# Placing the decoding of the second layer's weights: one or two units behind each f-tile's low part

## The chip, the cores and the metric

The kernel runs on one core of one Trainium2 chip. The metric is the device time of one execution in microseconds, as a median of several. TensorE (PE) does the matrix products, VectorE (DVE), ScalarE (ACT) and GpSimd (POOL) the elementwise work, and SyncE (SP) issues the transfers.

## The reference

Three stages follow one another. The first is attention with a hash mask (2 batches, 8 heads, 768 positions, head size 64). The second and the third are two gated layers over the 1536 resulting tokens of width 512:

```python
a = x @ w1            # 512 -> 1024
b = x @ w2
x = (a * b @ w3) @ w_out          # first layer; back to 512
gate = sigmoid(x @ w_gate)        # 512 -> 1536
val = x @ w_val
out = gate * val @ w_out2         # second layer; back to 512
```

The inputs are 64-bit floats. Each weight comes to the chip as raw 64-bit words and is turned into a 32-bit float there; this is called decoding.

## The kernel before

**Products.** A product of nearly 32-bit precision is made of three matmuls: each operand is split in a high and a low part, and `three` (line 698) sums high by high, high by low and low by high. A weight is split by `split_w` (line 686): ScalarE copies the high part, GpSimd (for the two first-stage weights) or VectorE (for the second-stage weight, `wt`) subtracts to get the low part.

**The loop.** During attention a generator already does the first layer for the first 512 tokens. The function `moe` (line 716) does the rest in 52 f-tiles, numbered n here: tiles 0 to 7 and 8 to 15 are the first layer for the second and third 512 tokens (8 f-tiles each), tiles 16 to 51 the second layer, 12 f-tiles for each 512 tokens. In its program order a tile n issues 12 matmuls into the PSUM tile `pa`, 12 into `pb`, then the split of its second-stage weight (line 786), and `post` (line 733): ScalarE copies `pa` into `a` (a sigmoid in the second layer, line 739), VectorE multiplies `pb` by it (line 741), ScalarE copies the high part `gh` (line 743), VectorE subtracts to get the low part `gl` (line 744). Then come the 12 matmuls of the second stage of the tile before, `second(n - 1)`, into four accumulators called `m` (line 793). At the end of each 512 tokens of the first layer, `second` also moves the four accumulators out, by ScalarE (line 763) and VectorE (line 764) into the tiles `x`. Last come this tile's decodes (lines 794 and 795) and the split of the first-stage weights of tile n + 1 (line 797).

**Decoding.** A unit is 128 by 512 weights. `decode` (line 323) first issues the load of the next unit on SP (`stage_next`, lines 310 to 321; four staging buffers `st` in two pools), and then for its own unit two ScalarE instructions (lines 334 and 335), one GpSimd instruction (line 336) and three VectorE instructions (lines 337, 338 and 343). Its work tiles `da` and `dr` have two buffers each in `moe`. The second layer has 36 units: 12 of `w_gate`, whose results go into the space of `xall`, then 12 pairs of `w_val` and `w_out2`, whose results go into the space of the first layer's weights, `w1r`, `w2r` and `wc`, once these are used up. Tile 16 + i of the second layer needs unit i of `w_gate` and pair i. The function `decodes(n)` gives two units to each odd n and one to each even n up to 24, 36 in all.

**Order.** The attention part is put in order by `order_engines`. The instructions of `moe` are put in order by the framework's scheduler: it simulates the program, and each engine takes the ready instruction that was written first. An instruction of `decode` can so be queued ahead of older work that is not ready yet, as far as its buffers allow. The order that comes out is fixed in each engine's queue, and each queue is worked off in order on the chip.

Of the kernel before, what the change touches and what calls it, by code (L numbers as in the profile page):

```python
# [16 lines left out]
ALU = mybir.AluOpType  # L17
# [211 lines left out]
def lsh_attention_moe_moe2_kernel(  # L229
# [36 lines left out]
    NF2 = FF2 // P  # L266
# [3 lines left out]
    dve = nc.vector  # L270
# [4 lines left out]
    def act_copy(dst, src):  # L275
        act.activation(out=dst, in_=src, func=AF.Copy)  # L276

    def f(ap):
        return ap.bitcast(F32)
# [27 lines left out]
    late = {}  # L307
    alt = [0, 0]

    def stage_next():  # L310

        if units:
            dst, src = units.pop(0)
            alt[0] += 1
            other = late.get("mp") or (wp if "mw" not in late else dec)
            t = (other if alt[0] % 2 else dec).tile([P, CH], U64, tag="st", name="st", bufs=2)
            shp = dst.shape
            ld = sync.dma_start(out=t if len(shp) == 2 else t.rearrange("p (k f) -> p k f", k=shp[1]), in_=src)
            if "c0" in late and alt[0] == 3:
                Tiles.holds.append((ld.ins.name, late["c0"].name))  # L320
            staged.append((dst, t))

    def decode():


        stage_next()
        dst, t = staged.pop(0)
        w = t[:, :].bitcast(U32).rearrange("p (n t) -> p n t", t=2)
        lw, hw = w[:, :, 0], w[:, :, 1]
        alt[1] += 1  # L330
        tp, nb = (late["mp"], 2) if "mp" in late else (wp if "mw" not in late and alt[1] % 2 else dec, 1)
        a = tp.tile([P, CH], U32, tag="da", name="da", bufs=nb)
        r = tp.tile([P, CH], I32, tag="dr", name="dr", bufs=nb)
        act.activation(out=f(a), in_=f(hw), func=AF.Abs)  # L334
        act.activation(out=r, in_=lw, func=AF.Copy, scale=2.0 ** -29)
        pool.tensor_scalar(out=f(a), in0=f(a), scalar1=F64_HI, scalar2=F64_LO, op0=ALU.min, op1=ALU.max)  # L336
        dve.tensor_scalar(out=a, in0=a, scalar1=3, scalar2=0x3FFFFFFF, op0=ALU.logical_shift_left, op1=ALU.bitwise_and)  # L337
        dve.scalar_tensor_tensor(out=a, in0=hw, scalar=0xC0000000, in1=a, op0=ALU.bitwise_and, op1=ALU.bitwise_or)  # L338
        ai, ri = a.bitcast(I32), r
        if len(dst.shape) == 3:  # L340
            ai = ai.rearrange("p (k f) -> p k f", k=dst.shape[1])
            ri = ri.rearrange("p (k f) -> p k f", k=dst.shape[1])
        dve.tensor_tensor(out=dst.bitcast(I32), in0=ai, in1=ri, op=ALU.add)  # L343
# [337 lines left out]
    def split_x(s, t, kcs):  # L681
        for kc in kcs:
            act_copy(t[0][:, kc], xraw[s][:, kc])
            dve.tensor_tensor(out=t[1][:, kc], in0=xraw[s][:, kc], in1=f(t[0][:, kc]), op=ALU.subtract)

    def split_w(pl, nm, src, bufs=2, eng=pool):
        hi = pl.tile([P, DM], F32R, tag=nm + "h", name=nm + "h", bufs=bufs)
        lo = pl.tile([P, DM], F32R, tag=nm + "l", name=nm + "l", bufs=bufs)
        shp = src.shape
        h3, l3 = hi, lo  # L690
        if len(shp) == 3:
            h3 = hi.rearrange("p (k f) -> p k f", k=shp[1])
            l3 = lo.rearrange("p (k f) -> p k f", k=shp[1])
        act_copy(h3, src)
        eng.tensor_tensor(out=l3, in0=src, in1=f(h3), op=ALU.subtract)  # L695
        return hi, lo
# [7 lines left out]
    def stage1(ps, w, x, kcs):  # L704
        for kc in kcs:
            three(ps, [t[:, kc * P:(kc + 1) * P] for t in w], [t[:, kc] for t in x], kc == 0, kc == KC - 1)

    def ftile(fi):

        ck, o = divmod(fi, KC)  # L710
        g = xall[:, o, ck * CH:(ck + 1) * CH].rearrange("p (k f) -> p k f", k=KC)
        if fi < NF1:
            return g, late["w1"][fi], late["w2"][fi].rearrange("p k f -> p (k f)")
        return g, wc[:, fi - NF1].rearrange("p (k f) -> p k f", k=KC), wc[:, fi - NF1 + KC]

    def moe(psM):


        tiles = [(1, s, fi) for s in range(1, NSW) for fi in range(NF1)] + [(2, s, fi) for s in range(NSW) for fi in range(NF2)]
        mp, mw = late["mp"], late["mw"]  # L720
        x2 = [(late["xh"], late["xl"])]
        x2 += [[mp.tile([P, KC, CH], F32R, name=f"x2_{i}_{t}") for i in range(2)] for t in range(1, NSW)]
        split_x(1, x2[1], range(KC))

        def weights(n):

            if n >= len(tiles):
                return None
            m, s, fi = tiles[n]
            ga, gb = (late["w1"][fi], late["w2"][fi]) if m == 1 else ftile(fi)[:2]  # L730
            return [split_w(mp, "wa", ga), split_w(mp, "wb", gb)]

        def post(n, ps):
            m, s, fi = tiles[n]
            a = mp.tile([P, CH], F32, tag="a", name="a", bufs=2)
            if m == 1:
                act_copy(a, ps[0])
            else:
                act.activation(out=a, in_=ps[0], func=AF.Sigmoid)
            gl = mw.tile([P, CH], F32R, tag="gl0", name="gl", bufs=2)  # L740
            dve.tensor_tensor(out=ps[1], in0=ps[1], in1=a, op=ALU.mult)  # L741
            gh = mw.tile([P, CH], F32R, tag="gh0", name="gh", bufs=2)
            act_copy(gh, ps[1])
            dve.tensor_tensor(out=gl, in0=ps[1], in1=f(gh), op=ALU.subtract)
            return gh, gl

        def second(n, g, wt, acc):
            m, s, fi = tiles[n]
            nf = NF1 if m == 1 else NF2
            last = n == len(tiles) - 1  # L750
            mm = None
            for c in range(4):
                cs = slice(c * P, (c + 1) * P)
                with tc.issue_after(mm.ins) if last and c else nullcontext():
                    if m == 1:
                        mm = three(acc[c], [t[:, cs] for t in wt], g, fi == 0, fi == nf - 1)
                    else:
                        mm = three(acc[c], [t[:, cs] for t in g], wt, fi == 0, fi == nf - 1)
            if fi < nf - 1:
                return  # L760
            for c in range(4):
                if m == 1:
                    act_copy(x2[s][0][:, c], acc[c])
                    dve.tensor_tensor(out=x2[s][1][:, c], in0=acc[c], in1=f(x2[s][0][:, c]), op=ALU.subtract)
                else:
                    o = mp.tile([P, DM], F32, tag="a" if last and c < 2 else "o", name="o", bufs=2)
                    if last and c % 2:
                        dve.tensor_copy(o, acc[c])
                    else:
                        act_copy(o, acc[c])  # L770
                    b, n = divmod(s * (CH // P) + c, NT)
                    sync.dma_start(out=out[b * S:(b + 1) * S].rearrange("(p c) d -> c p d", c=NT)[n], in_=o)

        ops = {0: weights(0), 1: weights(1)}
        gs, wts = {}, {}
        acc = None
        for n in range(len(tiles) + 1):
            if n < len(tiles):
                ps = [psM.tile([P, 512], F32, tag=t, name=t) for t in ("pa", "pb")]
                x = x2[tiles[n][1]]  # L780
                w = ops.pop(n)
                for kcs in ([range(KC)] if n else [range(KC - 1), range(KC - 1, KC)]):
                    for i in range(2):
                        stage1(ps[i], w[i], x, kcs)
                m, s, fi = tiles[n]
                wts[n] = split_w(mp, "wt", wc[:, fi] if m == 1 else ftile(fi)[2], eng=dve)
                gs[n] = post(n, ps)
            if n == 0:
                continue
            if acc is None:  # L790
                acc = [psT.tile([P, 512], F32, tag="t", name="m0"), psT.tile([P, 512], F32, tag="t", name="m1"),
                       psT.tile([P, 512], F32, tag="t", name="m2"), psT.tile([P, 512], F32, tag="t", name="m3")]
            second(n - 1, gs.pop(n - 1), wts.pop(n - 1), acc)
            for _ in range(decodes(n)):
                decode()
            if n + 1 < len(tiles):
                ops[n + 1] = weights(n + 1)
            if n == 3:
                split_x(2, x2[2], range(KC))

    def decodes(n):
        return 1 + n % 2 if n <= 24 else 0

    load_head(0, "qk")
    sync.dma_start(out=pq_raw[0:D], in_=proj)
# [126 lines left out]
```

## Time and profile before

| | us |
|---|---|
| median of 3 runs (843.55 to 844.79) | 844.46 |
| the profiled execution's own time | 844.29 |
| its span, from the first to the last instruction | 842.2 |
| PE busy / DVE busy / ACT busy / POOL busy in the span | 805.5 / 568.6 / 524.4 / 337.5 |

The profile was taken of one execution. Its rows name a line of the kernel, an engine, the operation and its tiles (output, then inputs). A matmul row names the moving operand first and the stationary one second. "Idle before" is the time for which an engine stood still ahead of an instruction, with what ended it. Stretches of time are counted from the start of the span.

### The profile page before, as it was taken

How to read it: one execution, taken by the hardware profiler on the slowest of the kernel's cores; microseconds unless marked ns; L12 is line 12 of the kernel's file. 1: busy time of each engine (PE TensorE's matmuls, PEld its weight loads, DVE VectorE, ACT ScalarE, POOL GpSimd, SP SyncE). 2: the span in 40 equal slices, each digit the busy share in tenths (PEclk: the TensorE clock that was granted, in tenths of full speed). 3: DMA queues.
4: the chain of work that ended last, by engine and by line, in shares of the span. 5: the costliest groups of instructions: out<-in, count | busy, mean ns of one | idle time of the engine just before them, and what ended most of it. 6: DMA issues, size and time to landing. Idle time of an engine off the chain costs nothing.

```text
span 842.2 us, 12220 instructions
## 1 busy us (share of the span) xinstructions
PE 805.5 (96%) x4272; PEld 682.6 (81%) x4272; DVE 568.6 (68%) x969; ACT 524.4 (62%) x1024; POOL 337.5 (40%) x329
## 2 busy tenths in 40 slices
PE   6889999999989999999999999999999999999998
PEld 5767878889878989888888677778888888888886
DVE  7999998888899889988399999962222222222222
ACT  5898877677788988777266765653334333343332
POOL 3466332142456352339444455443233333323330
PEclk9999999999999999999999999999999999999999
DMA  7666554344345444322024434300001000010001
GB/s 233 172 165 172 158 159 125 93 110 110 74 126 146 131 118 117 98 61 69 32 72 154 156 120 142 110 0 1 1 1 50 2 1 0 1 51 1 0 1 50
DMA packets 44748, 71.15 MB, mean 84 GB/s; under 512 B 6096, under 2 KB 32720, under 8 KB 44688
## 3 DMA queue, kind: packets, MB, share of 16 engines
q1 hardware_dynamic: 44688, 70.39, 28.7%
q8 instruction: 33, 0.54, 0.3%
q14 instruction: 27, 0.22, 0.1%
HBM read 52.43 MB, written 3.19 MB: 66 GB/s over the span
## 4 chain that ended last, share of the span: by engine, by line
PE 69%; DVE 15%; ACT 8%; issue 6%; DMA 1%; POOL 0%; DVEq 0%; ACTq 0%; POOLq 0%
PE pa L701 13%; PE m L701 12%; PE pb L701 12%; PE av L540 6%; PE tp L523 5%; PE p L701 4%; PE wacc L596 4%; PE s L469 3%; DVE da L338 3%; PE s L472 3%; DVE da L337 3%; PE y L701 3%; DVE pt L527 2%; PE gps L403 2%; ACT e L490 2%
## 5 line engine op out<-in xcount | busy, mean ns | idle before, releaser
L741 DVE TENSOR_TENSOR pb<-pb,a 128x512 f32<-128x512 f32 x52 | 36.2, 696 | 138.8 <-PE pb L701 134.8
L523 PE MATMUL tp<-idf,e 128*128 128x128 f32 x576 | 102.8, 276 | 5.5 <-DVE pt L527 4.3
L490 ACT ACTIVATE e<-s,sm 128x768 f32<-128x768 f32 x96 | 95.9, 999 | 15.2 <-DVE sm L480 13.0
L527 DVE TENSOR_TENSOR pt<-tp,pt 128x384 fp32r<-128x384 f32 x192 | 101.3, 549 | 5.9 <-ACT pt L526 4.3
L526 ACT ACTIVATE pt<-tp 128x384 fp32r<-128x384 f32 x192 | 90.5, 495 | 21.2 <-PE tp L523 19.3
L695 POOL TENSOR_TENSOR wal<-xall,wah 128x512 fp32r<-128x512 f32 x36 | 46.9, 1302 | 136.4 <-ACT wah L276 136.4
L336 POOL TENSOR_SCALAR da<-da 128x512 f32<-128x512 f32 x76 | 52.5, 692 | 119.3 <-ACT da L334 118.7
L701 PE MATMUL pa<-x,wah 128*128 128x512 f32 x320 | 99.3, 389 | 0.0
L479 DVE TENSOR_REDUCE s<-s 128x1 f32<-128x768 f32 x96 | 91.8, 956 | 11.0 <-PE s L472 10.8
L701 PE MATMUL pb<-x,wbh 128*128 128x512 f32 x320 | 98.5, 389 | 0.0
L523 PEld LDWEIGHTS tp<-idf,e 128*128 128x128 f32 x576 | 71.7, 141 | 17.6 <-DVE pt L527 5.8
L540 PE MATMUL av<-pt,spv 128*128 128x256 f32 x576 | 78.5, 286 | 1.0 <-DVE pt L527 0.9
L540 PEld LDWEIGHTS av<-pt,spv 128*128 128x128 f32 x576 | 72.0, 191 | 4.2 <-DVE pt L527 1.4
L334 ACT ACTIVATE da<-st 128x512 f32<-128x512 f32 x76 | 51.3, 675 | 37.6 <-DVE w1r L343 14.2
L469 PE MATMUL s<-ak,aq 128*128 128x384 f32 x192 | 62.1, 388 | 10.6 <-ACT e L490 10.5
L701 PEld LDWEIGHTS pa<-x,wah 128*128 128x128 f32 x320 | 60.1, 188 | 12.4
L701 PEld LDWEIGHTS pb<-x,wbh 128*128 128x128 f32 x320 | 60.1, 188 | 12.4
L338 DVE SCALAR_TENSOR_TENSOR da<-st,da 128x512 uint32<-128x512 uint32 x76 | 67.2, 884 | 1.5
L596 PE MATMUL wacc<-wo,t 128*128 128x512 f32 x192 | 65.4, 417 | 0.1
L701 PE MATMUL pa<-x,wal 128*128 128x512 f32 x160 | 62.3, 389 | 0.0
L701 PE MATMUL pb<-x,wbl 128*128 128x512 f32 x160 | 62.3, 389 | 0.0
L276 ACT ACTIVATE wah<-xall 128x512 fp32r<-128x512 f32 x36 | 22.8, 633 | 56.3 <-PE pa L701 56.2
(161 smaller groups left out, 1930.2 us busy)
## 6 DMA issues: line engine op xcount, KB each, us to landing
st<-in_moe_w_dram SPq DMA_DIRECT2D x32, 512.0 KB, 3.7
st<-in_moe_w_out_dram SPq DMA_DIRECT2D x20, 512.0 KB, 3.4
st<-in_moe_w_gate_dram SPq DMA_DIRECT2D x12, 512.0 KB, 3.5
st<-in_moe_w_val_dram SPq DMA_DIRECT2D x12, 512.0 KB, 3.5
rawq<-in_q_dram SPq DMA_DIRECT2D x16, 192.0 KB, 3.3
rawk<-in_k_dram SPq DMA_DIRECT2D x16, 192.0 KB, 3.3
rawv<-in_v_dram SPq DMA_DIRECT2D x16, 192.0 KB, 2.8
rr<-row SPq DMA_DIRECT2D x16, 192.0 KB, 3.3
```

Of the source, the lines that this page charges most:

```text
L334: act.activation(out=f(a), in_=f(hw), func=AF.Abs)
L336: pool.tensor_scalar(out=f(a), in0=f(a), scalar1=F64_HI, scalar2=F64_LO, op0=ALU.min, op1=ALU.max)
L338: dve.scalar_tensor_tensor(out=a, in0=hw, scalar=0xC0000000, in1=a, op0=ALU.bitwise_and, op1=ALU.bitwise_or)
L469: pe.matmul(s[:, half, :HS], lhsT=m["aq"][:, qs], rhs=m["ak"][:, ks], start=True, stop=False)
L479: dve.tensor_reduce(out=one[:, 1:2], in_=s[:, :, :HS], op=ALU.max, axis=AX.XY, negate=True)
L490: act.activation(out=e.rearrange("p (a c) -> p a c", a=2), in_=s[:, :, :HS], func=AF.Exp, bias=sm[:, 1:2], scale=sm[:, 0:1], accum_out=su_ ...
L523: pe.transpose(ps[:, j * P:(j + 1) * P], e[:, c * P:(c + 1) * P], idf)
L526: act.activation(out=dh, in_=src, func=AF.Copy)
L527: dve.tensor_tensor(out=lo[:, g % 2, half * 3:half * 3 + 3], in0=src, in1=f(dh), op=ALU.subtract)
L540: pe.matmul(acc[:, :2 * P].rearrange("p (a t) -> p a t", a=2), lhsT=w, rhs=r[:, :, c], start=(c == 0 and i == 0), stop=(c == NT - 1 and i ...
L596: pe.matmul(acc, lhsT=t3[x][:, j], rhs=wo[y][:, j], start=(j == 0 and n == 0), stop=(j == NF1 - 1 and n == 2))
L701: mm = pe.matmul(ps, lhsT=lhs[x], rhs=rhs[y], start=start and n == 0, stop=stop and n == 2)
```

## The change

The VectorE instruction that makes the low part `gl` of tile n is remembered. The decodes of tile n are traced in a block that orders each of their VectorE instructions behind it in VectorE's queue (an order of issue, not a wait for its end). The ScalarE, GpSimd and SP instructions of the decodes get no such edge. The number of decodes becomes one for tiles 1 to 12 and two for tiles 13 to 24, 36 in all again, in the same order of units.

```diff
-            dve.tensor_tensor(out=gl, in0=ps[1], in1=f(gh), op=ALU.subtract)
+            late["gl"] = dve.tensor_tensor(out=gl, in0=ps[1], in1=f(gh), op=ALU.subtract).ins
...
-            for _ in range(decodes(n)):
-                decode()
+            with tc.issue_after(late["gl"]):
+                for _ in range(decodes(n)):
+                    decode()
...
     def decodes(n):
-        return 1 + n % 2 if n <= 24 else 0
+
+        return 1 if n <= NF2 else 2 if n <= 2 * NF2 else 0
```

`NF2` is 12.

## Rows read from the trace of the kernel before

**Rows 1.** The page: busy time of the engines over the span.

```profile
PE 805.5 (96%) x4272; PEld 682.6 (81%) x4272; DVE 568.6 (68%) x969; ACT 524.4 (62%) x1024; POOL 337.5 (40%) x329
```

**Rows 2.** Busy time by stretches (header line names the columns).

```profile
core 0: us, PE busy (x) PEld busy (x) DVE busy (x) ACT busy (x) POOL busy (x), PEclk, DMA share, GB/s
426.10:470.00 43.90, 43.87 (x193) 35.86 (x192) 42.73 (x58) 28.14 (x51) 20.43 (x22) 1.00 0.43 135
470.00:558.20 88.20, 82.96 (x351) 64.50 (x350) 82.85 (x105) 56.83 (x103) 47.20 (x43) 1.00 0.34 112
558.20:838.40 280.20, 280.20 (x1237) 231.72 (x1235) 72.16 (x104) 104.77 (x177) 82.69 (x64) 1.00 0.02 9
```

**Rows 3.** Waits of PE, 426 to 558 us (us in total, times, longest).

```profile
PE m L701 <- DVE gl L744: 3.1, 5, 1.4
PE m L701 <- DVE x L764: 1.1, 1, 1.1
```

**Rows 4.** VectorE in order of time, 508 to 517 us (start, us, instruction).

```profile
508.05 0.69 DVE L741 TENSOR_TENSOR pb<-pb,a 128x512 f32<-128x512 f32 x1
508.65 0.68 DVE L343 CUSTOM_DVE_ANT_0 w2r<-da,dr 128x1024 uint16<-128x1024 uint16 x1
509.91 0.69 DVE L744 TENSOR_TENSOR gl<-pb,gh 128x512 fp32r<-128x512 f32 x1 [0.58 <-ACT gh L276]
510.52 0.68 DVE L695 TENSOR_TENSOR wtl<-wc,wth 128x512 fp32r<-128x512 f32 x1
511.12 0.84 DVE L337 TENSOR_SCALAR da<-da 128x512 uint32<-128x512 uint32 x1
511.99 0.69 DVE L338 SCALAR_TENSOR_TENSOR da<-st,da 128x512 uint32<-128x512 uint32 x1
512.60 1.52 DVE L337 TENSOR_SCALAR da<-da 128x512 uint32<-128x512 uint32 x1
514.15 1.66 DVE L338 SCALAR_TENSOR_TENSOR da<-st,da 128x512 uint32<-128x512 uint32 x1
...
516.34 0.69 DVE L741 TENSOR_TENSOR pb<-pb,a 128x512 f32<-128x512 f32 x1
```

**Rows 5.** The chain that ended last, around 564 us (start, us, what).

```profile
563.68 2.72 PE m L701 x12
```

**Rows 6.** VectorE in order of time, 563 to 568 us.

```profile
563.77 0.70 DVE L741 TENSOR_TENSOR pb<-pb,a 128x512 f32<-128x512 f32 x1 [4.01 <-issue]
565.14 0.69 DVE L744 TENSOR_TENSOR gl<-pb,gh 128x512 fp32r<-128x512 f32 x1 [0.67 <-ACT gh L276]
```

**Rows 7.** VectorE in order of time, single instructions at 437 and at 489 to 551 us.

```profile
437.41 0.41 DVE L337 TENSOR_SCALAR da<-da 128x512 uint32<-128x512 uint32 x1
...
489.83 0.69 DVE L741 TENSOR_TENSOR pb<-pb,a 128x512 f32<-128x512 f32 x1
...
499.24 0.69 DVE L741 TENSOR_TENSOR pb<-pb,a 128x512 f32<-128x512 f32 x1
...
551.47 1.19 DVE L343 CUSTOM_DVE_ANT_0 wc<-da,dr 128x1024 uint16<-128x1024 uint16 x1
```

**Rows 8.** GpSimd in order of time, 511 to 516 us.

```profile
511.04 0.63 POOL L336 TENSOR_SCALAR da<-da 128x512 f32<-128x512 f32 x1 [1.24 <-ACT da L334]
512.13 1.70 POOL L695 TENSOR_TENSOR wal<-w1r,wah 128x512 fp32r<-128x512 f32 x1 [0.46 <-ACT wah L276]
...
561.54 1.29 POOL L695 TENSOR_TENSOR wal<-xall,wah 128x512 fp32r<-128x512 f32 x1 [3.80 <-ACT wah L276]
```

**Rows 9.** Waits of SP's queue, 400 to 600 us (total, times, longest).

```profile
SPq L318 <- DVE da L338: 128.3, 31, 30.8
```

**Rows 10.** ScalarE in order of time, 546 to 548 us.

```profile
546.20 0.67 ACT L334 ACTIVATE da<-st 128x512 f32<-128x512 f32 x1 [1.42 <-DVE wc L343]
...
547.98 1.28 ACT L739 ACT_TABLE_LOAD   x1
```

## The prediction

> **What bounds the kernel now.** I began with the page: PE is busy for 805.5 us of 842.2 [rows 1], so the gain has to be sought where PE stands still. That share is too kind, because a matmul's modelled end overlaps the next one; I therefore counted matmuls per stretch instead of reading busy time. From 558.20 us to the end of the loop PE runs 1237 matmuls in 280.20 us, 0.2265 us each [rows 2]. That is its full pace: a tile of 36 matmuls takes 8.15 us, and the chain there consists of PE alone, a dozen matmuls each 2.72 us [rows 5]. At this pace the 351 matmuls of the stretch from 470 to 558.2 us would take 79.5 us; they took 88.2 [rows 2]. The 193 of the stretch before it would take 43.7 us and took 43.9. So decoding costs PE 8.7 + 0.2 = **8.9 us**, nearly all of it in some ten tiles, and nothing later.
>
> Who holds PE there? Its own waits name VectorE: the second stage `m` waits for `gl` five times and for the accumulators' move-out [rows 3]. VectorE is busy for 82.85 of the 88.2 us, against 72.16 of 280.2 us later [rows 2]. I then read one whole VectorE cycle [rows 4]. From one product on `pb` to the next it takes 8.29 us, holding two decode units (each one instruction of lines 337, 338 and 343) and the tile's own three instructions. In the quiet stretch a tile's product starts as soon as `pb` is done and `gl` ends 2.06 us later (563.77 to 565.83) [rows 6]. The second stage of that tile begins only three dozens of matmuls after 563.68, at 571.84 [rows 5]. VectorE can therefore run 6.0 us late before PE feels it. In the stretch of the loss that allowance is used up: two tiles took 9.41 us (489.83 to 499.24) and 8.81 us (499.24 to 508.05) on VectorE [rows 4, 7].
>
> **The change, part by part.** I take its parts against the profiled execution of 844.29 us, 0.17 us below the median of 844.46.
>
> *What stays.* The 36 units, their 36 loads and their order stay; only their place changes. Today the last unit ends at 552.7 us [rows 7]. From 563.68 us to the loop's end at 838.40 lie 274.7 us, 101 dozens of matmuls [rows 2, 5]: tile 17's `m`, three dozens for each of 33 more tiles, and tile 51's `m`. The `gl` that ends at 565.83 [rows 6] is therefore tile 18's, and tile 24's would end six tiles later, near 615 us by today's clock: decoding is spread over 60 us more, at a lower density.
>
> *Tiles 1 to 12, one unit.* VectorE's own work is 2.06 us from product to `gl`, plus 0.68 us for the low part of `wt` [rows 4, 6]. A unit that meets nobody takes 0.41 + 0.69 + 0.68 = 1.8 us [rows 4, 7]. That makes 4.5 us. If VectorE waited out every GpSimd instruction of the tile, two splits of 1.29 us and one clamp of 0.63 us [rows 8], it would be 7.7 us. Both ends are below 8.15 us, so nothing is lost here, not even with the move-out of tile 8 (four instructions of `gl`'s size, 2.8 us), which the 6.0 us cover.
>
> *Tiles 13 to 24, two units.* This is the unknown. The low end of a VectorE cycle is 2.06 + 0.68 + 3.6 = 6.3 us. The high end adds every GpSimd instruction, two splits and two clamps, 3.8 us: 10.1 us. The nearest row is the cycle that already holds two units, 8.29 us; its stretched instructions (0.84 and 1.52 us for line 337, 1.66 us for line 338, against 0.41 and 0.69) carry 2.5 us of such waiting [rows 4, 7]. I take 8.3 us. With c for the cycle, VectorE falls behind by c - 8.15 a tile, and once by 2.8 us for the move-out in tile 16; PE loses 12 x (c - 8.15) + 2.8 - 6.0 us, or nothing if that is negative. At 8.3 us the lag ends at 4.6 us, inside the allowance. The loss starts at c = 8.42.
>
> The stretching is two engines taking turns: a split lasts 1.70 us where VectorE decodes beside it, 1.29 us where it doesn't [rows 8]. The Trainium skill, SBUF — State Buffer, section "SBUF: two separate sides", has GpSimd and some VectorE instructions share a port that one holds to its end while the other is fully blocked. By that rule, if every GpSimd instruction met a decode, c would be the high end; the trace agrees that such waits happen, but shows 2.5 us of them and not 3.8.
>
> *What is queued behind the new edges.* The next tile's product stands behind two units on VectorE. For `gh` ScalarE waits for that product, then `gl`, then PE: this is the chain whose lateness the 6.0 us cover. The edge binds a unit to its own tile's `gl` only, so its last instruction may still fill the pause while ScalarE makes the next `gh`, as in [rows 4].
>
> *Other queues.* SP's 36 loads wait for staging buffers that line 338 frees, 128.3 us in all [rows 9]; they will wait longer, and nobody for them, as four buffers run ahead. ScalarE's two and GpSimd's one instruction per unit follow their two work buffers; they can be done while VectorE handles the tile's own work. If that cover is gone, VectorE waits for them, which is inside the 9.41 us cycle.
>
> *Deadlines.* Pair i is decoded in tile 13 + i and split for tile 16 + i, two tiles or 16 us later; the `w_gate` units have more. No stall of PE should come from here.
>
> *Sum.* 844.46 - 8.9 = 835.6. I leave 0.5 us for the move-out in tile 16, half of the 1.1 us that it cost PE before [rows 3], since it still meets two units: **836.1 us**. This case reaches from 834.6 (nothing lost, and the 0.9 us by which the fastest of the runs shown lies below their median) to 838 (the whole 1.1 us, and a tenth of a microsecond in each of the 12 tiles).
>
> **The rivals.**
> 1. *VectorE stays the bound in the two-unit tiles, and part of the gain is lost.* At c = 8.81 the loss is 4.7 us: 840.3. For it: that cycle stands in the trace with about two units. Against it: it was measured while VectorE was at the end of its allowance and held by full buffers.
> 2. *The same collision, worse, on the other side: slower.* Place: VectorE's queue in tiles 13 to 24, where GpSimd's splits meet two units in each tile. It decides at c = 9.16 us, where the loss reaches 8.9. At 9.41 us the loss is 11.9 us, 847.5; at the high end of 10.1 us it is 20 us, 856. For it: one cycle of 9.41 us with about two units [rows 7]. Against it: the following cycles shrink to 8.81 and 8.29 us.
> 3. *ScalarE must swap tables.* The sigmoid's table load comes at 547.98 us, after the last decode's absolute value at 546.20 [rows 10]; now nine tiles (16 to 24) hold both. ScalarE is busy for 56.83 us in 351 matmuls, 9.75 tiles [rows 2]: 5.8 us a tile. Two loads of 1.28 us a tile make 8.4 us, which the allowance absorbs; four make 10.9 us and lose 9 x 2.75 - 6 = 19 us: 854. No row shows an absolute value after the sigmoid's table, but copies go on under it with no further load. The Trainium skill, ScalarE: Activation LUTs, section "Table sets: the hidden batching unit", counts abs among the cheap functions that every set has; by that there is no swap.
> 4. *The change doesn't do what it says.* If the scheduler's order hardly moved, the time would be 844.5. Against it: the last unit cannot end at 552.7 us any more.
>
> **How the numbers follow.** Forecast 0.75, rival 1 0.12, rival 2 0.05, rival 3 0.02, rival 4 0.06 (with what else may eat the gain). The range takes the forecast's own lower edge, 834.6, and reaches through rival 1, to 841.0. A measurement of this kernel can tell about 0.2%, 1.7 us. Faster by more than that: forecast and rival 1, 0.87. Within it: 0.06. Slower: rivals 2 and 3, 0.07.
>
> **What would show it.** Right: PE in dozens of 2.72 us from 426 us on, no waits of `m` for `gl`; VectorE's busy share in the stretch up to 515 us falling to about two thirds, then high until some 610 us; products in tiles 13 to 24 starting ever later than `pb`'s end, but less than 6 us. Wrong: waits of `m` for `gl` between 515 and 615 us, VectorE cycles above 8.4 us there, more than two table loads on ScalarE, or PE waiting for a split weight in tiles 16 to 27.

## The result, and the profile after

| | before | after |
|---|---|---|
| median of 6 runs each, us | 844.75 (843.55 to 847.65) | 835.75 (834.55 to 837.17) |
| the profiled execution's own time / its span, us | 844.29 / 842.2 | 834.55 / 832.6 |

The ratio is 0.9885, with a 95% interval of 0.9869 to 0.99: 9.0 us less by the medians, against 8.4 us forecast and 8.9 us that the prediction gave as the most to be had. The next line is the page's busy time after, which answers to [rows 1].

```profile
PE 801.0 (96%) x4272; PEld 683.6 (82%) x4272; DVE 540.7 (65%) x969; ACT 523.9 (63%) x1024; POOL 332.0 (40%) x329
```

No instruction was added or taken away on any engine, yet VectorE is busy for 27.9 us less than before: its instructions became shorter. Where they did is seen below. Busy time by stretches, of the changed kernel, answers to [rows 2] and has its columns; the cuts are at 515 us, where the one-unit tiles end, and at 620 us, after the last unit.

```profile
426.10:470.00 43.90, 43.90 (x195) 36.38 (x194) 26.57 (x42) 23.71 (x41) 16.25 (x17) 1.00 0.25 80
470.00:515.00 45.00, 45.00 (x200) 37.25 (x200) 21.72 (x36) 24.88 (x44) 19.06 (x18) 1.00 0.19 63
515.00:620.00 105.00, 105.00 (x465) 86.96 (x464) 72.33 (x115) 63.22 (x113) 50.08 (x49) 1.00 0.30 101
620.00:829.00 209.00, 208.79 (x922) 172.57 (x920) 53.82 (x79) 78.37 (x132) 60.64 (x47) 1.00 0.03 12
```

The matmul counts, in brackets behind PE's busy time, say it all for PE: 860 matmuls in the first 193.9 us are 0.2255 us each, the full pace; before, the 351 from 470 to 558.2 us took 0.2513 us each [rows 2]. (A matmul that runs across a cut is counted on both sides of it; taken as one stretch the 193.9 us hold 857, 0.2263 us each.) VectorE's share is 0.61, 0.48, 0.69 and 0.26 in the four stretches; before it was 0.97 and then 0.94 up to 558 us [rows 2]. PE has no wait at all between 420 and 630 us, so nothing answers to [rows 3]. The chain that ended last (the work followed back from the last instruction) holds nothing but PE from 424 to 620 us:

```profile
by line: PE m L701 35.0%; PE pb L701 34.7%; PE pa L701 30.3%
```

VectorE in order of time, of the changed kernel, answers to [rows 4]: a two-unit tile on time (13), then the product and `gl` of tile 17, behind the move-out, and one of the later tiles (21).

```profile
513.38 0.70 DVE L741 TENSOR_TENSOR pb<-pb,a 128x512 f32<-128x512 f32 x1 [3.72 <-PE pb L701]
514.74 0.69 DVE L744 TENSOR_TENSOR gl<-pb,gh 128x512 fp32r<-128x512 f32 x1 [0.67 <-ACT gh L276]
515.35 0.75 DVE L337 TENSOR_SCALAR da<-da 128x512 uint32<-128x512 uint32 x2
516.02 1.29 DVE L338 SCALAR_TENSOR_TENSOR da<-st,da 128x512 uint32<-128x512 uint32 x2
517.22 0.69 DVE L695 TENSOR_TENSOR wtl<-wc,wth 128x512 fp32r<-128x512 f32 x1
517.82 0.69 DVE L343 CUSTOM_DVE_ANT_0 w1r<-da,dr 128x1024 uint16<-128x1024 uint16 x1
518.43 0.69 DVE L343 CUSTOM_DVE_ANT_0 w2r<-da,dr 128x1024 uint16<-128x1024 uint16 x1
521.54 0.70 DVE L741 TENSOR_TENSOR pb<-pb,a 128x512 f32<-128x512 f32 x1 [2.42 <-PE pb L701]
...
529.70 0.70 DVE L741 TENSOR_TENSOR pb<-pb,a 128x512 f32<-128x512 f32 x1 [2.00 <-PE pb L701]
...
547.97 0.69 DVE L741 TENSOR_TENSOR pb<-pb,a 128x512 f32<-128x512 f32 x1
550.87 0.69 DVE L744 TENSOR_TENSOR gl<-pb,gh 128x512 fp32r<-128x512 f32 x1 [2.21 <-ACT gh L276]
...
580.78 0.70 DVE L741 TENSOR_TENSOR pb<-pb,a 128x512 f32<-128x512 f32 x1 [0.97 <-ACT a L739]
582.90 0.69 DVE L744 TENSOR_TENSOR gl<-pb,gh 128x512 fp32r<-128x512 f32 x1 [1.42 <-ACT gh L276]
...
588.62 0.70 DVE L741 TENSOR_TENSOR pb<-pb,a 128x512 f32<-128x512 f32 x1 [0.99 <-ACT a L739]
```

Tile 13 takes 8.16 us, of which VectorE stands still for 0.67 + 2.42 us: it does the same two units and its own three instructions in 5.07 us. In [rows 4] the same work took 8.29 us with 0.58 us of standing still. Tile 21 takes 7.84 us with 1.42 + 0.99 us of waiting for ScalarE, so 5.43 us of work. Between them, tile 17's `gl` is one of the two latest (tile 19's is as late): its product, two tiles after the punctual one at 529.70, was due at 529.70 + 16.30 = 546.00 and its `gl` 2.06 us later, at 548.06; it ended at 551.56, 3.5 us late. By the prediction's estimate PE can bear 6.0.

The costliest groups of VectorE show the shortening per unit. First the kernel before, 470 to 558.2 us, then the changed one, 513 to 613 us (columns: busy us and mean ns, then idle time before).

```profile
L338 DVE SCALAR_TENSOR_TENSOR da<-st,da 128x512 uint32<-128x512 uint32 x22 | 22.8, 1038 | 0.6
L337 DVE TENSOR_SCALAR da<-da 128x512 uint32<-128x512 uint32 x22 | 18.5, 843 | 0.5 <-POOL da L336 0.5
```

```profile
L338 DVE SCALAR_TENSOR_TENSOR da<-st,da 128x512 uint32<-128x512 uint32 x24 | 16.5, 689 | 0.4
L337 DVE TENSOR_SCALAR da<-da 128x512 uint32<-128x512 uint32 x24 | 10.8, 453 | 0.0
```

With line 343 (918 ns before, 758 ns after, as a mean over its three destinations) a unit costs 2.80 us before and 1.90 us after; one that meets nobody takes 1.8 [rows 4, 7]. The three instructions are the same ones. Finally ScalarE in order of time, with its only load of a table in the loop, which answers to [rows 10]:

```profile
536.16 1.28 ACT L739 ACT_TABLE_LOAD   x1
537.46 0.60 ACT L739 ACTIVATE a<-pa 128x512 f32<-128x512 f32 x1
537.95 0.65 ACT L334 ACTIVATE da<-st 128x512 f32<-128x512 f32 x1
...
578.51 0.68 ACT L334 ACTIVATE da<-st 128x512 f32<-128x512 f32 x1 [2.95 <-DVE w1r L343]
...
580.17 0.58 ACT L739 ACTIVATE a<-pa 128x512 f32<-128x512 f32 x1
```

The absolute value of line 334 follows the sigmoid with no further load. The last two rows belong to tile 21: `a` comes late because it is queued behind a decode, for whose work buffer, freed by line 343, ScalarE waited 2.95 us.

### The profile page after: what moved, and what is told of

Its sections match the earlier page's. It is cut to its first block, busy times and chain, and to the rows that moved or that the text cites. A ratio compares the mean times of both kernels' runs of the same rounds, so it can differ in the third digit from the quotient of the medians.

```text
span 832.6 us, 12204 instructions
## 1 busy us (share of the span) xinstructions
PE 801.0 (96%) x4272; PEld 683.6 (82%) x4272; DVE 540.7 (65%) x969; ACT 523.9 (63%) x1024; POOL 332.0 (40%) x329
## 4 chain that ended last, share of the span: by engine, by line
PE 84%; DVE 8%; ACT 5%; issue 1%; DMA 1%; POOL 0%; SPq 0%; ACTq 0%; DVEq 0%; POOLq 0%
PE m L701 17%; PE pb L701 17%; PE pa L701 17%; PE av L540 6%; PE tp L523 5%; PE p L701 5%; PE wacc L596 4%; PE s L469 3%; PE s L472 3%; PE y L701 3%; PE gps L403 2%; DVE pt L527 2%; DVE s L479 1%; PE trr L391 1%; ACT pt L526 1%
## 5 line engine op out<-in xcount | busy, mean ns | idle before, releaser
L744 DVE TENSOR_TENSOR gl<-pb,gh 128x512 fp32r<-128x512 f32 x52 | 36.0, 691 | 40.0 <-ACT gh L276 40.0
L472 PE MATMUL s<-bk,bq 128*128 128x384 f32 x192 | 57.2, 359 | 0.3 <-DVE bq L453 0.3
```

What stands on the lines that cost most here:

```text
L472: pe.matmul(s[:, half, :HS], lhsT=m["bq"][:, qs], rhs=m["bk"][:, ks], start=False, stop=True)
```

## The experiments

My theory was that the edge keeps VectorE from being filled with units, so that its lateness stays inside PE's allowance. Two things had to be told apart: whether the edge or the new counts did it, and whether the loss of before was simply too much work on VectorE or its collisions with GpSimd. The counts without the edge need no run: with them each engine's queue comes out the same as before, instruction by instruction, since the scheduler takes a unit as early as its buffers allow, whichever tile it was written in.

**The edge alone, with the old counts.**

```diff
-        return 1 if n <= NF2 else 2 if n <= 2 * NF2 else 0
+        return 1 + n % 2 if n <= 24 else 0
```

> The edge behind gl stays, the number of units per tile is that of the kernel before (two in odd tiles, one in even ones, tiles 1 to 24). Theory A (the edge does it: it keeps a unit from running ahead into a tile whose VectorE work is full, and at one and a half units a tile VectorE's cycle stays under 8.15 us): no waits of m for gl, 835 to 836.5 us, the same as the changed kernel. Rival B (the thinning to one and then two units does it): units crowd as in the kernel before, 841 to 845 us. Rival C (units must come late, in tiles 13 to 24): part of the loss stays, 838 to 842 us.

It took 835.92 us (834.21 to 836.47), 0.9885 of before [0.987, 0.9899], the same as the change, and PE has no wait in the loop. So the edge is what works: the old counts with it gain all, and the new counts without it leave the queues as they were. Two units in each odd tile, from the first tiles on, are as harmless as two in every late tile.

**The edge on the product instead of on `gl`.** The units may then be queued in the pause in which ScalarE makes `gh`.

```diff
-            dve.tensor_tensor(out=ps[1], in0=ps[1], in1=a, op=ALU.mult)
+            late["gl"] = dve.tensor_tensor(out=ps[1], in0=ps[1], in1=a, op=ALU.mult).ins
...
-            late["gl"] = dve.tensor_tensor(out=gl, in0=ps[1], in1=f(gh), op=ALU.subtract).ins
+            dve.tensor_tensor(out=gl, in0=ps[1], in1=f(gh), op=ALU.subtract)
```

> The changed kernel's counts, but the edge starts at the tile's product on pb instead of at gl, so units may run between the product and gl. Theory A (only VectorE's work per tile and 6.0 us of allowed lateness count): gl comes up to about 3.5 us later in two-unit tiles, inside the allowance, 835 to 837 us. Rival C (the exact place behind gl matters, because a unit ahead of gl holds back the chain product, gh, gl): 839 to 844 us, with waits of m for gl.

It took 835.82 us (835.02 to 837.8), 0.989 [0.9873, 0.9907], again without a wait of PE. For the time it matters that a unit belongs to its tile; its exact place in the tile does not. For the price of a unit the place does matter. In tile 12, with one unit, line 337 behind the product starts while GpSimd splits `wb`, and lasts 1.44 us; in the changed kernel, behind `gl`, that split is over, and it lasts 0.42 us. First this run, then the changed kernel:

```profile
509.08 1.29 POOL L695 TENSOR_TENSOR wbl<-w2r,wbh 128x512 fp32r<-128x512 f32 x1 [1.43 <-ACT wbh L276]
509.22 1.44 DVE L337 TENSOR_SCALAR da<-da 128x512 uint32<-128x512 uint32 x1
```

```profile
505.69 1.29 POOL L695 TENSOR_TENSOR wbl<-w2r,wbh 128x512 fp32r<-128x512 f32 x1 [1.05 <-ACT wbh L276]
507.19 0.42 DVE L337 TENSOR_SCALAR da<-da 128x512 uint32<-128x512 uint32 x1
```

From 513 to 613 us, in the tiles with two units, a unit costs 2.47 us here and 1.90 in the changed kernel, though VectorE pauses here too (1.63 us in the tile from 582.05 us on). Two such units still fit: that tile's other 6.53 us are all of VectorE's work.

**Two a tile, earlier and past both move-outs.**

```diff
-        return 1 if n <= NF2 else 2 if n <= 2 * NF2 else 0
+        return 2 if n <= 6 or 8 < n <= 20 else 0
```

> The edge stays; two units a tile in tiles 1 to 6 and 9 to 20 (36 in all), so the pairs come four tiles earlier than in the changed kernel, in the very tiles in which the kernel before lost its time. Theory A (two units a tile behind the edge give a VectorE cycle under 8.15 us or a little over it, wherever they stand): 835 to 837 us and no waits of m for gl. Rival C (the time was lost because of the tiles, the end of the first layer with its splits, not because of the crowding): 839 to 844 us.

It took 837.56 us (834.99 to 837.91), 0.9906 [0.9885, 0.9927]. Between 420 and 640 us PE has one wait, the row below; in the matmul counts 0.9 us are missing (395 in the 90 us from 425 us on, where the two kernels above have 399). The median lies a little above the 835 to 837 us of theory A, which had also excluded any such wait, and below the 839 to 844 of rival C. So the early tiles themselves don't cause the loss of before: two units fit there too, but for some 0.8 us (the loop's time, at the end of this section).

```profile
PE m L701 <- DVE gl L744: 0.2, 1, 0.2
```

**Three a tile.** So that the weights come in time, the units are put in the order gate, value, output of one f-tile, and all are decoded in tiles 13 to 24.

```diff
         for i in range(NF2):
             units.append((ftile(i)[0], kpf(w_gate, i * P, P)))
-        for i in range(NF2):
             units.append((ftile(i)[1], kpf(w_val, i * P, P)))
...
-        return 1 if n <= NF2 else 2 if n <= 2 * NF2 else 0
+        return 3 if NF2 < n <= 2 * NF2 else 0
```

> The edge stays; all 36 units move into tiles 13 to 24, three a tile (w_gate, w_val and w_out2 of one f-tile together). Theory A prices a unit by the changed kernel's trace, 1.6 us undisturbed: a VectorE cycle of 2.06 + 0.6 + 4.8 = 7.5 us, up to 8.5 us where one or two splits of GpSimd are met; loss 12 x (c - 8.15) + 2.8 - 6.0, that is 0 to 1 us: 835.5 to 837 us. Rival D (a unit costs what it cost in the kernel before, 2.5 to 2.9 us): a cycle of 10.2 to 11.4 us, loss 21 to 36 us, 857 to 871 us.

It took 844.19 us (842.61 to 846.06), 0.9984 [0.9974, 0.9995]: neither of the forecasts, and almost the whole gain gone. The waits of PE from 420 to 640 us, and busy time of the 115 us from 515 us on (columns as above; with one line less in the kernel, most line numbers of its rows are one lower, here and in the two runs that follow):

```profile
PE m L700 <- ACT gh L276: 5.6, 5, 2.6
PE pb L700 <- ACT wbh L276: 0.7, 1, 0.7
```

```profile
515.00:630.00 115.00, 108.61 (x471) 87.71 (x470) 108.08 (x145) 76.02 (x133) 54.21 (x56) 1.00 0.45 146
```

PE does 471 matmuls where the edge alone does 509 in the same stretch: 38 x 0.2265 = 8.6 us. VectorE is busy for 0.94 of it, as before the change. In order of time it looks like this, tile 18 to 19, with the GpSimd split beside it in the second fence:

```profile
560.24 0.69 DVE L740 TENSOR_TENSOR pb<-pb,a 128x512 f32<-128x512 f32 x1
...
563.66 1.67 DVE L343 CUSTOM_DVE_ANT_0 w1r<-da,dr 128x1024 uint16<-128x1024 uint16 x1
...
567.32 1.72 DVE L343 CUSTOM_DVE_ANT_0 w2r<-da,dr 128x1024 uint16<-128x1024 uint16 x1
...
569.29 0.68 DVE L740 TENSOR_TENSOR pb<-pb,a 128x512 f32<-128x512 f32 x1
```

```profile
563.40 1.38 POOL L694 TENSOR_TENSOR wal<-xall,wah 128x512 fp32r<-128x512 f32 x1 [0.31 <-ACT wah L276]
...
567.20 1.28 POOL L694 TENSOR_TENSOR wbl<-w1r,wbh 128x512 fp32r<-128x512 f32 x1 [0.46 <-ACT wbh L276]
```

Each split has a decode instruction of 0.69 us beside it that lasts 1.0 us longer: it ends 0.55 us after the split, as if it had begun only behind it. A unit costs 2.51 us here, and nine cycles, 531.80 to 616.41, take 9.40 us each. Each tile adds 1.25 us of lateness. PE's first wait, the first row below, is for `gh`, which `m` needs ahead of `gl`. The product behind it, at 579.08, is 579.08 - 531.80 - 5 x 8.15 = 6.5 us late, and `gh` ends 1.84 us after that product (580.92) in place of 1.33 us in the quiet stretch (563.77 to 565.10, the last row, of the kernel before), so `gh` is 7.0 us late. PE waits 2.6 us: 4.5 us were free.

```profile
580.97 0.50 PE L700 MATMUL m<-wth,gh 128*128 128x512 f32 x1 [2.59 <-ACT gh L276]
...
580.32 0.60 ACT L276 ACTIVATE gh<-pb 128x512 fp32r<-128x512 f32 x1
```

```profile
564.50 0.60 ACT L276 ACTIVATE gh<-pb 128x512 fp32r<-128x512 f32 x1 [0.32 <-DVE pb L741]
```

The kernel before shows why. There `gh` is ready 571.84 - 565.10 = 6.7 us ahead of its `m` (the prediction's 6.0 us are the same count for `gl`). In the triples' PE queue `m` begins after two of the matmuls of `pb`, ten matmuls or 2.3 us sooner, which leaves 4.4 us. Theory A's forecast would have needed units that stay near 1.9 us at three a tile.

**Four a tile.** Same order of units.

```diff
-        return 3 if NF2 < n <= 2 * NF2 else 0
+        return 4 if NF2 < n <= NF2 + 9 else 0
```

> As the run with three units, but four a tile in tiles 13 to 21. Theory A: a cycle of 9.1 us undisturbed to 10.1 us, loss 9 x (c - 8.15) + 2.8 - 6.0 = 5 to 14 us: 841 to 850 us, with waits of m for gl from about tile 16 on. Rival D (the price of before): a cycle of 12.7 to 14.3 us, loss 38 to 52 us: 874 to 888 us. If VectorE's density did not matter at all once the edge is there: 835 to 836.5 us.

It took 843.73 us (842.58 to 845.23), 0.9987 [0.9977, 0.9996], with the same waits of PE (5.7 us of `m` for `gh` in place of 5.6). But the queue that came out still holds about three units a tile, as the two work buffers allow no more ahead. So it repeats the triples and says nothing of four.

**The triples, with GpSimd's splits on VectorE.** Were VectorE simply full, more work on it would lose more. Were the loss the two engines' turns, taking GpSimd's splits away would give it back.

```diff
-            return [split_w(mp, "wa", ga), split_w(mp, "wb", gb)]
+            eng = dve if 14 <= n < 27 else pool
+            return [split_w(mp, "wa", ga, eng=eng), split_w(mp, "wb", gb, eng=eng)]
```

> As the run with three units a tile, but the low parts of the first-stage weights of tiles 14 to 26 are subtracted by VectorE instead of GpSimd: VectorE gets 2 x 0.6 = 1.2 us a tile more to do and meets 2.6 us a tile less of GpSimd's work. Theory E (VectorE's units are slow at three a tile because they and GpSimd's splits take turns): the cycle falls from 9.4 to 8.0 to 8.6 us and the time to 835.5 to 839 us, although VectorE does more. Rival F (VectorE is simply full): the cycle grows to 10.6 us, the time to 852 to 858 us.

It took 837.4 us (836.59 to 838.71), 0.9912 [0.9894, 0.993]. Waits of PE in the loop, and the stretch from 515 us:

```profile
PE pb L700 <- ACT wbh L276: 0.8, 1, 0.8
```

```profile
515.00:630.00 115.00, 114.21 (x504) 94.25 (x503) 110.19 (x176) 81.09 (x142) 29.70 (x38) 1.00 0.46 147
```

VectorE does 176 instructions instead of 145, and PE gets 504 matmuls instead of 471. A unit costs 2.07 us instead of 2.51, and ten cycles, 531.59 to 615.51, take 8.39 us each instead of 9.40, two splits more in each. 6.8 us of the medians come back by giving the fuller engine more to do: theory E's range, and far from rival F's 852 to 858.

**The kernel before, with the splits on VectorE and no edge.** The same question at the loss itself.

```diff
-            return [split_w(mp, "wa", ga), split_w(mp, "wb", gb)]
+            eng = dve if 3 <= n < 18 else pool
+            return [split_w(mp, "wa", ga, eng=eng), split_w(mp, "wb", gb, eng=eng)]
```

> The kernel before, with the first-stage low parts of tiles 3 to 17 on VectorE instead of GpSimd: 1.2 us a tile more for VectorE, 2.6 us a tile less of GpSimd's work in its way. Theory E (turns with GpSimd make the crowded tiles of the kernel before slow): its cycles of 8.3 to 9.4 us fall to 7 to 8.3, the time to 835.5 to 840 us. Rival F (VectorE is simply full): cycles of 9.5 to 10.6 us, the time 853 to 860 us. In between, about 844 us, if both weigh the same.

It took 835.55 us (834.29 to 837.18), 0.9895 [0.9873, 0.9918], against 845.32 for before in the same series: as fast as the change, by another way. Busy time from 425 to 560 us:

```profile
425.00:560.00 135.00, 135.00 (x597) 111.81 (x596) 122.46 (x193) 92.78 (x161) 32.75 (x41) 1.00 0.36 117
```

VectorE is almost as full as before (0.91 of the stretch against 0.95), and PE stands still nowhere. A unit costs 2.10 us instead of 2.80. The crowding is the same as before: nine VectorE cycles in a row hold 22 units in both, and take 8.91 us each before (470.66 to 550.87 us) and 8.34 us each here (463.99 to 539.02 us), with two splits more in each. That is still 0.2 us above PE's 8.15, which makes nine cycles 1.7 us late, inside the allowance. So the loss of before was the time that VectorE and GpSimd spent waiting for each other in cycles that hold 2.4 units on average; VectorE's own work fits, with little to spare. Either remedy is enough: the edge with at most two units a tile, or the splits on VectorE.

The Trainium skill, Perfetto Trace Analysis, section "Optimizing Scalar/DVE Operations", says that moving work between GpSimd and VectorE might not help, as they share a read port. Here the measurement differs: the move gave 1.1%, as each 1.29 us split [rows 8] became a VectorE instruction of 0.68 to 0.72 us on average.

**Nine more instructions per tile in the quiet stretch**, in 8 tiles (the edit below) or in 16 (`n < 44`), to measure how late VectorE may be. They rewrite a product that has already been used, which no result needs.

```diff
+            if 28 <= n < 36:
+                for _ in range(9):
+                    dve.tensor_tensor(out=ps[1], in0=ps[1], in1=f(gh), op=ALU.subtract)
```

> The changed kernel; in the second layer's tiles 28 to 35, where nothing is decoded, VectorE gets nine more instructions of gl's size behind gl (they rewrite the spent product in PSUM, no result uses it). They follow one another at about 0.72 us, 6.5 us a tile, which makes a VectorE cycle of 2.06 + 0.6 + 6.5 = 9.2 us. Theory A (PE feels VectorE's lateness only past 6.0 us): 8 x 1.0 - 6.0 = 2 us lost, 837.5 to 838.5 us. Rival G (no allowance, each late microsecond is lost): 8 us, 843 to 845 us. Rival H (VectorE is not what holds PE): 835 to 836.5 us.

> As the run with eight such tiles, but in tiles 28 to 43, sixteen of them. Theory A: 16 x 1.0 - 6.0 = 10 us lost, 845 to 847 us, that is 8 us more than with eight. Rival G: 16 us, 851 to 853 us, also 8 us more than with eight, but 8 us from the start. Rival H: 835 to 836.5 us.

They took 836.71 us (834.62 to 837.55), 0.989 [0.986, 0.992], and 836.77 us (836.46 to 837.52), 0.9897 [0.9865, 0.9929]; PE has no wait in either. Rival G falls. Theory A's 845 to 847 us for sixteen tiles is missed by 8 us, and the times come nearest to rival H's; but neither is tested, as VectorE's cycle did not become as long as planned. The scheduler sees the extra instructions and puts some of PE's groups of `pa` ahead, and part of the extras fill the pause before `gl`. In the longer one 14 cycles, 645.88 to 766.13, take 8.59 us each and not 9.2, and 13 of the 15 products in them wait for `pb`, as in this row:

```profile
699.53 0.70 DVE L741 TENSOR_TENSOR pb<-pb,a 128x512 f32<-128x512 f32 x1 [0.43 <-PE pb L701]
```

VectorE was hardly behind there. That PE does wait once it is too far behind is shown by the triples; their 4.5 us for `gh` agree with the 4.4 us counted for it. The 6.0 us for `gl` were not put to a test by themselves.

**The loop alone.** From its first to its last matmul of `m` (their starts) the loop takes, in the profiled executions:

| | us |
|---|---|
| before | 411.90 (426.11 to 838.01) |
| the change; the edge alone; the edge on the product; splits on VectorE, no edge; eight tiles with extras | 402.33 to 402.34 |
| sixteen tiles with extras | 402.38 |
| two a tile, earlier | 403.09 |
| three a tile, splits on VectorE | 403.44 |
| three a tile; four a tile | 410.85; 410.88 |

Five kernels agree to 0.01 us here, while their profiled executions took 834.29 to 837.80 us: these differences arise ahead of the loop, which begins at 425.64 to 429.46 us, and say nothing about the decodes.

## Why the prediction was right, step by step

- **The pool of 8.9 us**, counted in matmuls, was about right and somewhat small. The loop is shorter by 411.90 - 402.33 = 9.57 us (the table above; the first `m` starts at 426.07 us after the change), and PE has no wait left in it; the medians differ by 9.0 us. Part of the shortfall is in the counting: the two stretches of [rows 2] both count the matmuls that run across their cut at 470 us, and 426.10 to 558.20 us taken as one stretch holds 542 and not 544, a loss of 9.3 us.
- **Who held PE**: VectorE, as read, but by its collisions. (Two further waits of `m` in the view behind [rows 3] name ScalarE, for the move-out's copy `x`, 0.7 us, and for `gh`, 0.4 us.) The prediction knew of the stretching (2.5 us in one cycle) and took it as a fixed part of a tile with two units. The runs show two things in its place. The cycles of the loss hold more than two units on average, 22 in nine cycles. And the price of a unit goes with what GpSimd does beside it: 2.80 us before, 1.90 after, 2.47 with the edge on the product, 2.10 when the splits leave GpSimd.
- **The mis-sized term is c.** Taken as 8.3 us from the nearest row [rows 4], it came out as 5.74 us on time (8.16 less the 2.42 us of waiting for `pb`) and 7.84 us in tile 21, where 2.4 us of it are waiting for ScalarE. The row came from a stretch in which VectorE had fallen behind and its decodes ran beside GpSimd's splits. The prediction's low end was the better guide: 6.3 us with all durations, which overlap by some 0.08 us from one instruction to the next. That c was too long did no harm to the forecast, as every c below 8.42 gives the same time. By the Trainium skill's rule of the shared port (SBUF — State Buffer, "SBUF: two separate sides") c would have been 10.1 if every GpSimd instruction met a decode; the trace agrees with the rule where they meet (1.44 us for line 337 beside a split of 1.29, above). Behind `gl` few of them meet.
- **The lag.** Forecast to grow to 4.6 us at tile 24, the product's lag peaked at 2.8 us at tile 18 (2.5 of it from the two tiles of the move-out, 9.88 + 8.95 us, forecast 3.1), that of `gl` at 3.5 us at tiles 17 and 19, where ScalarE's `gh` was late as well; from tile 20 on it shrank by some 0.3 us a tile. The 0.5 us reserved for the move-out weren't needed, which is about the difference from 836.1.
- **A small surprise in the cover**: in tiles 20 to 24 the product waits about 1 us for ScalarE's `a`, as shown above. Line 343 frees a work buffer, ScalarE decodes into it and then makes `a`, and VectorE goes on to its next units: this ring turns in 7.84 us, below PE's 8.15, and so costs nothing. The prediction had allowed for VectorE waiting for the decode's other engines; it waited for the tile's own sigmoid, queued behind a decode.
- **The rivals.** 1 and 2 needed c of 8.8 and more with two units; no cycle outside the move-out was that long. The triples show that their mechanism is real, at a density one unit higher: 9.40 us a tile, and most of the gain lost. 3 fell with the one table load; the Trainium skill, ScalarE: Activation LUTs, "Table sets: the hidden batching unit", had it so, and the trace agrees. 4 would have been true of the counts alone; with the edge the queue did change.
- **The signs named**: PE in dozens, no wait for `gl` and no third table load were there. One sign of being wrong came too, VectorE cycles above 8.4 us between 515 and 615 us, but only the two of the move-out, 9.88 and 8.95, whose lateness the allowance took. The products did not start ever later up to tile 24. VectorE's share up to 515 us was 0.54 (48.29 of 88.9 us), not two thirds, and 0.69 and not high up to 620 us, for the same reason as c. Deadlines and SP's loads cost nothing.

## What to carry to other kernels

An engine off the critical path that works in order, and that is handed optional work as early as buffers allow, fills up, and then every instruction of the path queues behind it: tie the optional work to the tile whose pause can hold it. Don't price the new arrangement with durations from the crowded stretch; take them from instructions that meet nobody, and count the meetings separately, by what the other engine does at that point of the tile. Before calling an engine full, move the other party's instructions away or onto it: if it becomes faster with more to do, it was waiting, not working.

## What was unexpected

Collisions between VectorE and GpSimd depend on where in the tile a unit stands, and not only on how many instructions there are: with the same counts and the same splits a unit costs 1.90 us behind `gl` and 2.47 behind the product, and VectorE pauses in both. Pauses alone don't prevent them. The instructions that grow are the decode's (line 337 from 0.41 to 1.52 us and line 338 from 0.69 to 1.66 [rows 4, 7], line 343 from 0.69 to 1.72) and VectorE's own split of `wt`, from 0.68 to 1.78 us at 543.87 us in the changed kernel, where GpSimd's split runs from 543.77 to 545.10. The tile's own product and `gl`, which read PSUM, keep their 0.68 to 0.70 us in every row shown. And three units a tile lose almost as much as the kernel before did, though two behind the edge lose next to nothing at either price: with two, VectorE's work of 5.1 to 6.5 us leaves a pause in a tile of 8.15 us; with three it has none.
